# A chunked-state burst one matrix product earlier in each later token group, and one state cast on another engine

## The chip, the cores and the metric

The kernel runs on one core of a Trainium2 chip. The metric is the device time of one execution in microseconds (us); the figure for a kernel is the median over its runs.

## The reference

Two parts follow each other. The first is a retention layer (attention without a softmax, with a decay by distance), the second a two-layer network with a leaky rectifier:

```python
scores = scale * np.matmul(q, k.transpose(0, 1, 3, 2))      # 8 batches, 8 heads, 576 tokens, 64 wide
ret = np.matmul(scores * Dmat, v)                            # Dmat = gamma_h ** (i - j) for i >= j, else 0
x = ret.transpose(0, 2, 1, 3).reshape(4608, 512)
h = x @ w_in                                                 # 512 -> 2048
out = np.maximum(0.01 * h, h) @ w_out                        # 2048 -> 512
```

## The kernel before

**Units and groups.** The 4608 tokens are cut into 36 units of 128 tokens (two chunks of 64), and four units make a group of 512 tokens; there are nine groups, g = 0 to 8. Retention is computed by units in chunked form: inside a chunk with masked scores, across chunks with a running state of 64 x 64 per head. The two layers are computed by groups. In group g the matrix products of the layers are issued together with the retention of the units that later groups need. All orders on all engines are written out by hand: `tc.manual_schedule()` is on, and every engine runs its instructions in the order in which the program issues them.

**One unit's retention.** `step(u)` is `burst(u)` and then the preparation of later units. `burst(u)` issues, on TensorE, `scores(u)` (lines 221 and 230, 64x64 tiles into the one tile `sc`: the pool has a single buffer) and `outputs(u - 1)` (lines 305 and 316, into the one tile `ot`, again a single buffer). Then on VectorE `masks(u)` (line 248, reads `sc`), `state(u, 0)` and `state(u, 1)` (lines 270 to 275, read and sometimes write `sc`), on GpSimd `state_cast(u)` (line 287, the fp16 copy `st` of the states), on ScalarE `own(u - 1)` (line 372, reads `ot`), and on VectorE `add(u - 1)` (line 377, reads `ot` and `own`, writes the transposed layer input `xT`). So `scores(u)` may write `sc` only when `masks(u - 1)` and both `state(u - 1)` have read it, and `outputs(u - 1)` may write `ot` only when `add(u - 2)` has read it. `outputs(u - 1)` also reads the `st` of unit u - 1. After the burst `fetch(u + 4)` issues loads on SyncE's queue, and `ahead(u + 2)` casts k on ScalarE, q and v on GpSimd, and issues a transposing transfer on SyncE's queue. When u is a multiple of four, `ahead` has `sum_x` between the casts of q and v: four GpSimd operations (line 457) on the finished `xT` of the next group, whose results the next group's first layer reads.

**The layers.** Each is computed with seven half-size products where eight would be plain (a Strassen-like scheme), so sums of operands and of results are needed. `h_seven` is the first layer (its products are line 470, and the plain blocks `h_block` between them line 390); `seven` is the second one (products at line 590, 16 matmuls each). The second layer's plan in `others` is, for groups 2 and later:

```python
("p1", ..., False, lambda: give(0, 0, "p1")),
("p6", ..., True,  lambda: keep("u2", "p6", "k1")),
("p5", ..., True,  lambda: keep("v", "p5", "u2")),
("p7", ..., True,  lambda: give(1, 1, "p7", "v")),
("p5", ..., False, lambda: give(0, 1, "p5", "u2")),
("p7", ..., False, lambda: give(1, 0, "p7", "u2")),
```

`keep` (line 604) and the `give` with a `plus` (line 616) are VectorE additions that read a product's PSUM tile. The fifth product adds into the tile that `keep("v")` has read, and the sixth into the tile that `give(1, 1)` has read, so each must wait for that read. Ahead of the plan VectorE computes the last operand sums, `mix(g, 3, ...)` (line 571). `hooks[n]` is what is issued after product n and its reader, `hooks[0]` after the two `mix`. The four steps of group g are step 5 and step 6 inside the two `h_seven`, step 7 at `hooks[0]` and step 8 at another hook of `others`; "step n" is the step of unit 4g + n. Groups 2 to 7 have these steps; in group 7, step 8 is unit 36, which doesn't exist, and only `outputs(35)`, `own(35)`, `add(35)` and `sum_x(8)` are left of it. After the plan comes the next group's `h_seven`, in which the third product reads the results of `sum_x`.

**Unit 7.** The first units are written out one by one. Between `scores(7)` and `finish2(7)` (which is `outputs(7)`, `own(7)` and `add(7)`) stand the states of unit 7; `outputs(7)` reads both `st` of unit 6 (second half) and of unit 7 (first half).

Of the kernel before, what the change touches and what calls it, by code (L numbers as in the profile page):

```python
# [18 lines left out]
def kernel(  # L19
# [217 lines left out]
    def masks(u, aside=False):  # L237
        s16s[u] = b_pool.tile([P, 2, NP, CH], F16, name="s16")
        if aside:
            nc.scalar.copy(out=s16s[u], in_=sc_tiles[u][:, :, 0])  # L240
            nc.gpsimd.tensor_tensor(  # L241
                out=s16s[u],
                in0=s16s[u],
                in1=mask16.unsqueeze(1).unsqueeze(1).to_broadcast([P, 2, NP, CH]),
                op=MUL,
            )
            return
        nc.vector.tensor_tensor(  # L248
            out=s16s[u],
            in0=sc_tiles[u][:, :, 0],  # L250
            in1=mask_sb.unsqueeze(1).unsqueeze(1).to_broadcast([P, 2, NP, CH]),
            op=MUL,
        )
# [3 lines left out]
    def state(u, j):  # L257

        if j == 0:
            s32s[u] = a_pool.tile([P, 2, NP, CH], FP, name="s32")  # L260
            st16[u] = a_pool.tile([P, 2, NP, CH], F16, name="st16")
        c = (2 * u + j) % CB
        if c == CB - 1:
            carry[0] = None
            return
        st = sc_tiles[u][:, j, 1]
        to = s32s[u][:, j]
        scaled = c % (BLK // CH) == BLK // CH - 1
        if carry[0] is None:
            nc.vector.tensor_copy(out=to, in_=st)  # L270
        elif not scaled:
            nc.vector.tensor_tensor(out=to, in0=st, in1=carry[0], op=ADD)  # L272
        else:
            nc.vector.tensor_tensor(out=st, in0=st, in1=carry[0], op=ADD)  # L274
            nc.vector.tensor_tensor(
                out=to, in0=st,
                in1=gblk_sb.unsqueeze(2).to_broadcast([P, NP, CH]), op=MUL,
            )
        carry[0] = to

    def live(u, j):
        return (2 * u + j) % CB != CB - 1

    def state_cast(u, copy, js=(0, 1)):
        js = [j for j in js if live(u, j)]
        if len(js) == 2:
            copy(out=st16[u], in_=s32s[u])  # L287
        else:
            for j in js:
                copy(out=st16[u][:, j], in_=s32s[u][:, j])  # L290
# [85 lines left out]
    def add(u):  # L376
        nc.vector.tensor_tensor(  # L377
            out=x_of(u).rearrange("q (c g) t -> q c g t", g=2),
            in0=ot_tiles[u][:, :, NP : 2 * NP].rearrange("q g (c j) t -> q c g (j t)", j=2),
            in1=owns[u].rearrange("q (c g) j t -> q c g (j t)", g=2),  # L380
            op=ADD,
        )
# [23 lines left out]
    def h_block(g, f):  # L406
        hps = acc_pool.tile([P, 1, TOK], FP, name="acc")
        h_mm(hps, 0, g, f, slice(0, TOK))
        leaky(g_tile(g)[:, f : f + 1, :], hps)
# [149 lines left out]
    def mix(g, n, x):  # L559

        fs = slice(x * HF // 2, (x + 1) * HF // 2)
        if g not in sums:
            sums[g] = s_pool.tile([P, 2, HF, HT], F16, name="mix")
        s = sums[g]
        z, a, b, op = (
            (s[:, 0], g_part(g, 1, 0), g_part(g, 1, 1), ADD),
            (s[:, 1], s[:, 0], g_part(g, 0, 0), SUB),
            (g_part(g, 1, 0), g_part(g, 0, 0), g_part(g, 1, 0), SUB),
            (g_part(g, 0, 0), g_part(g, 0, 1), s[:, 1], SUB),
        )[n]  # L570
        nc.vector.tensor_tensor(out=z[:, fs], in0=a[:, fs], in1=b[:, fs], op=op)
# [97 lines left out]
    pool_copy, act_copy, dve_copy = nc.gpsimd.tensor_copy, nc.scalar.copy, nc.vector.tensor_copy  # L669
# [155 lines left out]
    def step(u, split=False):  # L825
        rest = burst(u, True, split)
        if u > 13:
            fetch(u + 4)
        ahead(u + 2, (lambda: sum_x(u // 4 - 1)) if u % 4 == 0 else None)
        return rest  # L830
# [53 lines left out]
    own(6)  # L884
    state_cast(6, act_copy, (1,))
    state(7, 0)
    masks(7)
    add(6)
    state_cast(7, dve_copy, (0,))
    state(7, 1)  # L890
    halves(1, (0, 5), (0, 6))
    finish2(7)
# [42 lines left out]
    first, others = seven(1)  # L935
# [10 lines left out]
    for g in range(2, NG):  # L946
        more = g < NG - 1
        first, others = seven(g, not more)

        def block(f):  # L950
            return lambda: h_block(g, f)

        def at_step(n, split=False):
            return (lambda: step(4 * g + n, split)) if more else None

        owed = h_seven(
            g, 0, [block(2), block(10), block(3), block(11)], at_step(5, True)
        )
        owed += [lambda: mix(g, 0, 0), lambda: mix(g, 1, 0)]
        for late in h_seven(  # L960
            g, 4, [block(6), block(7), block(14), first], at_step(6, True), owed
        ):
            late()
        mix(g, 2, 0)
        h_block(g, 15)
        for n in range(3):
            mix(g, n, 1)
        others({0: [at_step(7)], 4: [at_step(8)]} if more else {})


# [28 lines left out]
```

## Time and profile before

| | |
|---|---|
| median of 13 runs | 284.37 us (284.13 to 286.36) |
| profiled execution: its own time | 284.37 us |
| profiled execution: span of the program | 282.6 us |
| TensorE matmul busy | 274.4 us, 97% |
| VectorE (DVE) busy | 211.5 us, 75% |
| ScalarE (ACT) busy | 153.1 us, 54% |
| GpSimd (POOL) busy | 156.0 us, 55% |
| TensorE clock granted | full, in every slice |

A row of the timeline is "start us, us, engine line operation written<-read, shapes, count, [idle before <- what ended it]". Lines that follow each other of one kind are merged. PE is TensorE, DVE VectorE, ACT ScalarE, POOL GpSimd, SP SyncE. A matmul's row lasts until its modelled end, some 0.17 us after its successor has begun, so TensorE's progress is read from starts, not from ends. A VectorE instruction can begin some 0.08 us before the end of the one ahead of it.

### The profile page before, as it was taken

The page shows a single profiled execution, that of the slowest core. Times are in us where ns is not written, and L with a number is a line of the kernel's source. Part 1 is how long each engine was busy: PE and PEld are TensorE (multiplying, and loading weights), DVE is VectorE, ACT ScalarE, POOL GpSimd, SP SyncE. Part 2 cuts the span into 40 slices and gives each one's busy share as a digit, 9 for nine tenths or more (in the row PEclk, how much of TensorE's full clock was granted, in tenths as well). Part 3 has the DMA queues.
Part 4 walks back from the last instruction along what each step waited for, and adds up shares of the span by engine and source line. Part 5 has one row for each costly group of instructions (what it writes and reads, how often), then busy time and mean ns, then how long its engine had stood idle before and what let it go on. Part 6 is the DMA issues. An engine that isn't in the chain of part 4 may idle for free.

```text
span 282.6 us, 9823 instructions
## 1 busy us (share of the span) xinstructions
PE 274.4 (97%) x4229; PEld 205.6 (73%) x4229; DVE 211.5 (75%) x362; ACT 153.1 (54%) x282; POOL 156.0 (55%) x173
## 2 busy tenths in 40 slices
PE   7889999999999999999999999999999999999994
PEld 3568888745876787678867886788678867886683
DVE  2875688988866887689777986788688767865772
ACT  3766787633237733774277427752775277416610
POOL 8969755944459507950795069607951693051000
PEclk9999999999999999999999999999999999999999
DMA  8999999998999767987698669966996251012004
GB/s 221 297 245 205 291 207 315 232 198 195 237 266 287 167 137 107 281 191 173 144 272 184 151 116 296 189 152 142 249 208 152 50 179 39 2 74 77 0 3 148
DMA packets 123100, 50.04 MB, mean 177 GB/s; under 512 B 112048, under 2 KB 116784, under 8 KB 123056
## 3 DMA queue, kind: packets, MB, share of 16 engines
q1 hardware_dynamic: 116032, 37.23, 57.6%
q0 software_dynamic: 6736, 12.06, 17.7%
q8 instruction: 33, 0.54, 0.8%
q10 hardware_dynamic: 288, 0.11, 0.1%
q14 instruction: 11, 0.09, 0.1%
HBM read 36.81 MB, written 9.44 MB: 164 GB/s over the span
## 4 chain that ended last, share of the span: by engine, by line
PE 90%; DVE 6%; DMA 2%; issue 1%; ACT 0%; POOL 0%; DVEq 0%; POOLq 0%
PE acc L590 35%; PE acc L390 27%; PE acc L470 15%; PE acc L527 5%; PE sc L221 3%; DMA t<-in_q_dram 2%; PE ot L305 2%; PE ot L316 2%; PE sc L230 2%; DVE s L248 1%; DVE s L272 1%; PE acc L202 1%; DVE qk L177 1%; DVE st L290 1%; DVE sc L274 0%
## 5 line engine op out<-in xcount | busy, mean ns | idle before, releaser
L390 PE MATMUL acc<-xT,w_in 128*128 128x256 f16 (+2 forms) x496 | 88.6, 318 | 0.1
L590 PEld LDWEIGHTS <-gt 128*128 128x128 f16 x640 | 61.3, 98 | 8.5 <-ACT gt L404 0.8
L404 ACT ACTIVATE gt<-acc 128x512 f16<-128x512 f32 x102 | 58.4, 597 | 14.2 <-PE acc L390 13.5
L390 PEld LDWEIGHTS <-w_in 128*128 128x128 f16 x496 | 45.4, 98 | 17.8 <-issue 0.2
L590 PE MATMUL acc<-w_out,gt 128*128 128x256 f16 x384 | 46.3, 273 | 0.2 <-ACT gt L404 0.2
L372 ACT COPY own<-ot 128x512 f32<-128x512 f32 x33 | 19.3, 586 | 41.1 <-PE ot L316 40.9
L287 POOL CAST st<-s 128x512 f16<-128x512 f32 x21 | 12.8, 610 | 48.9 <-DVE s L272 31.2
L177 POOL TENSOR_TENSOR qk<-t,cs 128x512 f16<-128x512 f32 x28 | 30.7, 1096 | 0.1
L181 POOL TENSOR_TENSOR v<-t,cs 128x512 f16<-128x512 f32 x28 | 30.7, 1098 | 0.0
L590 PE MATMUL acc<-w_mix,gt 128*128 128x256 f16 x256 | 30.6, 273 | 0.0
L590 PE MATMUL acc<-w_mix,mix 128*128 128x256 f16 x256 | 29.3, 273 | 0.0
L404 ACT ACTIVATE gt<-h 128x512 f16<-128x512 f32 x42 | 25.7, 629 | 5.7 <-DVE h L481 5.3
L470 PEld LDWEIGHTS <-w_sum 128*128 128x128 f16 x224 | 21.9, 98 | 9.1 <-issue 1.1
L590 PEld LDWEIGHTS <-mix 128*128 128x128 f16 x256 | 25.0, 98 | 3.0
L377 DVE TENSOR_TENSOR xT<-ot,own 128x512 f16<-128x512 f32 x33 | 22.5, 681 | 3.0 <-ACT own L372 3.0
L481 DVE TENSOR_TENSOR h<-acc,u 128x512 f32<-128x512 f32 x28 | 19.2, 684 | 6.4 <-PE acc L470 6.4
L241 POOL TENSOR_TENSOR s<-s,idle 128x512 f16<-128x512 f16 x12 | 13.9, 1156 | 16.9 <-ACT s L240 16.9
L174 ACT CAST qk<-t 128x512 f16<-128x512 f32 x36 | 22.5, 625 | 1.1 <-DMA t<-in_k_dram 0.9
L470 PE MATMUL acc<-x_sum,w_sum 128*128 128x256 f16 x168 | 22.9, 272 | 0.0
L481 DVE TENSOR_TENSOR u<-acc,k 128x512 f32<-128x512 f32 x14 | 9.7, 690 | 17.4 <-PE acc L470 14.8
L470 PEld LDWEIGHTS <-w_in 128*128 128x128 f16 x168 | 16.3, 97 | 7.1 <-DVE h L481 0.8
L488 ACT COPY k<-acc 128x512 f32<-128x512 f32 x14 | 8.2, 585 | 22.1 <-issue 16.8
(77 smaller groups left out, 434.2 us busy)
## 6 DMA issues: line engine op xcount, KB each, us to landing
out_dram<-osb SPq DMA_DIRECT2D x17, 512.0 KB, 3.8
t<-in_k_dram SPq DMA_DIRECT2D x24, 256.0 KB, 3.7
t<-in_q_dram SPq DMA_DIRECT2D x23, 256.0 KB, 4.2
t<-in_v_dram SPq DMA_DIRECT2D x22, 256.0 KB, 4.8
t<-in_v_dram POOLq DMA_DIRECT2D x10, 256.0 KB, 6.4
t<-in_q_dram POOLq DMA_DIRECT2D x9, 256.0 KB, 5.7
t<-in_k_dram POOLq DMA_DIRECT2D x8, 256.0 KB, 7.4
w_in<-in_moe_w_in_dram POOLq DMA_DIRECT2D x8, 256.0 KB, 6.8
```

The lines of the kernel that those rows point to most:

```text
L174: nc.scalar.copy(out=qk16[u][:, 1], in_=t32[u, 1])
L177: eng.tensor_tensor(out=qk16[u][:, 0], in0=t32[u, 0], in1=decay(u, 0), op=MUL)
L181: eng.tensor_tensor(out=v16[u], in0=t32[u, 2], in1=decay(u, 1), op=MUL)
L241: nc.gpsimd.tensor_tensor(out=s16s[u], in0=s16s[u], in1=mask16.unsqueeze(1).unsqueeze(1).to_broadcast([P, 2, NP, CH]), op=MUL,)
L372: nc.scalar.copy(out=owns[u], in_=ot_tiles[u][:, :, 0:NP].rearrange("q j c t -> q c j t"))
L377: nc.vector.tensor_tensor(out=x_of(u).rearrange("q (c g) t -> q c g t", g=2), in0=ot_tiles[u][:, :, NP : 2 * NP].rearrange("q g (c j) t -> ...
L390: nc.tensor.matmul(out=hps[:, n, :], lhsT=w_in16[:, c, f * P : (f + 1) * P], rhs=xT[g][:, c, ts], start=(c == 0), stop=(c == NP - 1),)
L404: nc.scalar.activation(out=out, in_=in_, func=mybir.ActivationFunctionType.Lrelu)
L470: nc.tensor.matmul(out=r[name][:, n, :], lhsT=lhs[:, c, n * P : (n + 1) * P], rhs=rhs[:, c, :], start=fresh and n == 0 and c == 0, stop=c ...
L481: nc.vector.tensor_tensor(out=r[name], in0=r[a], in1=r[b], op=ADD)
L527: nc.tensor.matmul(out=ys[tb], lhsT=g_t[0][:, f, tb * P : (tb + 1) * P], rhs=w_out16[:, f, :], start=(f == 0), stop=(f == NF - 1),)
L590: nc.tensor.matmul(out=r[name][tb][:, 0, :] if apart else r[name][0][:, tb, :], lhsT=lhs[:, f, tb * P : (tb + 1) * P], rhs=rhs[:, f, :], s ...
```

## The change

Two edits. In the loop over groups 2 to 8, step 8 goes from the hook after the fourth product of the second layer to the hook after the third. In the part written out by hand, the fp16 cast of the first state of unit 7 goes from VectorE, behind `masks(7)` and `add(6)`, to ScalarE, ahead of them.

```diff
     own(6)
     state_cast(6, act_copy, (1,))
     state(7, 0)
+    state_cast(7, act_copy, (0,))
     masks(7)
     add(6)
-    state_cast(7, dve_copy, (0,))
     state(7, 1)
     halves(1, (0, 5), (0, 6))
     finish2(7)
...
         for n in range(3):
             mix(g, n, 1)
-        others({0: [at_step(7)], 4: [at_step(8)]} if more else {})
+        others({0: [at_step(7)], 3: [at_step(8)]} if more else {})
```

Each engine's order changes in this way. On TensorE the burst of step 8 (64 matmuls of 64x64) stands ahead of the fourth product's 16 matmuls instead of behind them. On VectorE `give(1, 1)` stands behind the burst's masks, two states and addition instead of ahead of them; the two `keep` stay ahead of the burst. On ScalarE, GpSimd and SyncE's queue the order in the loop stays as it was. For unit 7 VectorE has one instruction less and ScalarE one more.

## The prediction

> **What bounds the kernel now.** I read the page first. TensorE is busy nearly all the time, VectorE three quarters of it, and the clock is full.
>
> ```profile
> span 282.6 us, 9823 instructions
> ...
> PE 274.4 (97%) x4229; PEld 205.6 (73%) x4229; DVE 211.5 (75%) x362; ACT 153.1 (54%) x282; POOL 156.0 (55%) x173
> ...
> PEclk9999999999999999999999999999999999999999
> ...
> PE 90%; DVE 6%; DMA 2%; issue 1%; ACT 0%; POOL 0%; DVEq 0%; POOLq 0%
> ```
>
> The fourth line is the chain that ended last: 90% TensorE. So a moved burst pays only where it takes a wait off TensorE, and costs what new waits it puts there. TensorE's matmul count doesn't change.
>
> Next I read the windows view over the second layer, from the first `mix(g, 3)` to `give(0, 1)`, in groups 2 to 5, and for comparison a stretch of the first layer (columns: stretch, its length, busy time of each engine with instructions).
>
> ```profile
> 100.10:110.70 10.60, 10.60 (x156) 9.35 (x155) 10.19 (x18) 2.69 (x6) 3.68 (x5) 1.00 0.62 91
> 128.70:139.20 10.50, 10.50 (x156) 9.25 (x155) 10.10 (x18) 2.67 (x5) 3.73 (x5) 1.00 0.58 131
> 157.30:167.80 10.50, 10.50 (x156) 9.26 (x154) 10.13 (x18) 2.63 (x5) 3.64 (x5) 1.00 0.59 112
> 185.70:196.20 10.50, 10.50 (x156) 9.26 (x154) 10.10 (x18) 2.70 (x6) 3.70 (x5) 1.00 0.57 129
> ...
> 110.00:120.00 10.00, 10.00 (x130) 6.71 (x128) 6.09 (x11) 6.54 (x12) 9.92 (x11) 1.00 1.04 258
> ```
>
> The third figure after the length is VectorE: 10.10 of 10.50 us. VectorE is full just where the burst is moved, and has slack elsewhere. Last, the timeline of group 3 there (step 7 is unit 19, step 8 unit 20), VectorE's rows and then TensorE's:
>
> ```profile
> 133.37 0.42 DVE L275 TENSOR_TENSOR s<-sc,cs 128x256 f32<-128x256 f32 x1
> 133.72 0.68 DVE L377 TENSOR_TENSOR xT<-ot,own 128x512 f16<-128x512 f32 x1
> 134.31 0.68 DVE L604 TENSOR_TENSOR u<-acc,k 128x512 f32<-128x512 f32 x1
> 135.10 0.69 DVE L604 TENSOR_TENSOR v<-acc,u 128x512 f32<-128x512 f32 x1
> 135.88 0.69 DVE L616 TENSOR_TENSOR osb<-acc,v 128x512 f32<-128x512 f32 x1
> 136.49 0.68 DVE L248 TENSOR_TENSOR s<-sc,cs 128x512 f16<-128x512 f32 x1
> 137.09 0.87 DVE L272 TENSOR_TENSOR s<-sc,s 128x256 f32<-128x256 f32 x2
> 137.87 0.68 DVE L377 TENSOR_TENSOR xT<-ot,own 128x512 f16<-128x512 f32 x1
> ```
>
> ```profile
> 133.43 1.91 PE L590 MATMUL acc<-w_mix,gt 128*128 128x256 f16 x16
> 135.26 0.32 PE L221 MATMUL sc<-qkT 64*64 64x64 f16 x16
> 135.41 0.30 PE L230 MATMUL sc<-v,qk 64*64 64x64 f16 x16
> 135.54 0.30 PE L305 MATMUL ot<-s,v 64*64 64x64 f16 x16
> 135.67 0.31 PE L316 MATMUL ot<-qkT,st 64*64 64x64 f16 x16
> 135.91 1.92 PE L590 MATMUL acc<-w_out,gt 128*128 128x256 f16 x16
> 137.66 1.91 PE L590 MATMUL acc<-w_mix,gt 128*128 128x256 f16 x16
> ```
>
> The reader is to see three things. The fourth product begins at 133.43, which is where the burst is to go. At that moment VectorE hasn't yet done `state(19, 1)` (to 133.79) and `add(18)` (133.72 to 134.40), which free `sc` and `ot`. And the burst at 135.26 has all it needs in the order as it is.
>
> **The moved burst, group 3.** Spacings from starts: a product takes 1.75 us (135.91 to 137.66), 1.83 ahead of a burst (133.43 to 135.26); scores to outputs 0.28; outputs to the next product 0.37. Without waits the moved scores would start at 133.43 + 0.08 = 133.51, outputs at 133.79, the fourth product at 134.16. How fast TensorE goes on after such a wait I take from two bursts that stand one product apart at 70 us: there `state` ended at 70.26 and scores began at 70.41 (0.15), `add` ended at 70.86 and outputs began at 70.91 (0.05). So scores start at 133.79 + 0.15 = 133.94, outputs at the later of 134.22 and 134.40 + 0.05 = 134.45. The cast of `st` (to 134.54) is wanted by the second half of the far outputs, at about 134.65: in time. The fourth product starts at 134.45 + 0.37 = 134.82, 0.66 late.
>
> Then VectorE: `v` ends at 135.79; the burst's masks follow at once, at 135.71 with the usual overlap instead of 136.49 (0.78 earlier), since `give(1, 1)` no longer stands ahead. `add(19)` goes from 137.87 to 137.09, and `give(1, 1)` behind it runs 137.69 to 138.38. On TensorE the fifth product starts at 134.82 + 1.75 = 136.57 (it needs `v`: there), the sixth would at 138.32 but needs `give(1, 1)`: 138.38 + 0.05 = 138.43. The next group starts at 140.18, where it now starts at 139.41: 0.77 later.
>
> What it gains: `sum_x` follows `add` and the q cast on GpSimd, so it too comes 0.78 earlier, and the third product of the next `h_seven` waits for it now. The block ahead of that product takes 0.87 us elsewhere, but in groups 2 to 7 it lasts 1.01, 0.93, 1.06, 0.91, 0.86 and 0.86: waits of 0.14, 0.06, 0.19, 0.04, 0 and 0. With the next group late and `sum_x` early, all go. Net for group 3: 0.77 - 0.06 = 0.71.
>
> **The other groups,** by the same steps (fourth product's start T; `add` of step 7 ends; outputs start; `give(1, 1)` ends; next group's start now and then). Group 2: T 104.84, `sc` free 105.34, `add` 105.94, outputs 105.99, fourth product 106.36; `give` ends 109.93, so the sixth starts 109.98 instead of 109.86; 110.88 becomes 111.73, +0.85 - 0.14 = 0.71. Group 4: T 161.99, `add` 162.49, outputs 162.54, fourth product 162.91; three state operations make `give` end at 167.07, so the sixth waits from 166.41 to 167.12; 167.97 becomes 168.87, +0.90 - 0.19 = 0.71. Group 5: T 190.47, `add` 190.95, fourth product 191.37, `give` 195.41, sixth 195.46; 196.46 becomes 197.21, +0.75 - 0.04 = 0.71. That the four agree is no accident: now and then VectorE's one sequence sets the end. Group 6: one state operation less in step 7, `add` ends at 218.84 with outputs due at 219.15, `give` at 222.82 with the sixth due at 223.02: 0. Group 7: only outputs, due 247.15, `add` 247.71, outputs 247.76, all behind 0.59 late and no wait to gain: 252.79 becomes 253.38, +0.59. Sum: 4 x 0.71 + 0.59 = 3.43 us. Each group's VectorE sequence starts behind a leaky rectifier of that group (0.58 us idle before the first `mix`), so it moves with TensorE and doesn't catch up.
>
> **What else moves.** Step 8's own copy (0.59), the k cast (0.62) and GpSimd's casts stand in the same order and only come earlier; ScalarE sat idle 5.4 us ahead of that copy. SyncE's three loads and one transposing transfer of step 8 come up to 1.75 us earlier, with no transfer overtaken in the queue; their data are wanted one or more steps later, so 0. If the DMA share (0.6 in these windows) made them collide, GpSimd's casts would be late, with a whole step of cover.
>
> **The cast of unit 7.** Now `outputs(7)` waits for it: that run of line 316 lasts 0.47 us where the like lasts 0.32. On ScalarE the cast takes 0.41 (its row for this shape) and fits at 43.0 to 43.4, ahead of a rectifier that starts at 43.48 and waits for TensorE anyway. Gain 0.15, cost 0; if it pushed that rectifier, 0.1 lost at most.
>
> **Total:** 3.43 - 0.15 = +3.28. The profiled execution's own time, 284.37, is the median, so 287.65; I say 287.6.
>
> **Two rules of the Trainium skill against these rows.** "Perfetto Trace Analysis", section Identifying the Most-Contended Engine, takes an engine's occupancy over the window as a fair measure of its load. Over the span VectorE's 75% would leave a quarter free, the burst's 64 matmuls would find their tiles free, and the sum would be -0.43 - 0.15 = -0.6. The windows say 96%, and the stage decides. "TensorE: Matmul & The Clock Gate", section The HAM clock gate, halves TensorE's clock after an idle window of some 3.4 us, and its oscillation section tells of micro-idling that does it too. In this trace TensorE sits idle 0.65 us ahead of 15.8 and 0.51 ahead of 10.1, and PEclk stays at 9. I take no loss; by the rule a throttled window per stalled group would be an estimated 3.4/2 x 5 = 8.5 us more.
>
> **Rivals.** (a) VectorE keeps up: if `add` and `give(1, 1)` came 0.7 us earlier, as in group 6, no wait arises, `sum_x` is early, and the kernel goes to 284.4 - 0.6 = 283.8. It decides from the point where `add` of step 7 ends before T + 0.36. Against it: five of six groups miss that (group 7, without scores, T + 0.08) by 0.12 to 0.74 us. (b) Only the wait inside the burst counts, because `give(1, 1)` isn't in the sixth product's way: fourth products late by 0.79, 0.66, 0.19, 0.17, 0 and 0.59, less 0.43, 0.15 and the 0.06 that group 2's fifth product waits now: +1.8, 286.1. (c) The clock: 296. (d) As forecast, but each wait costs 0.15 more than I took, some seven waits: 288.7.
>
> **How the numbers follow.** Forecast with small deviations 0.70; (b) 0.11; (d) 0.08; (c) 0.02; (a) 0.09. Measurement tells about 0.3%, 0.85 us, from no change; (a) lies inside, with 0.03 beyond. So faster 0.03, same 0.06, slower 0.91. The range 286.1 to 288.8 holds the forecast, (b)'s value and (d).
>
> **What would show it.** Right: fourth products late behind line 305 waiting for DVE L377, sixth behind L616 in groups 2, 4 and 5, none in group 6; no wait for POOL x_sum; line 316 of unit 7 back at 0.32 us; each of groups 2 to 5 longer by 0.7. Wrong: outputs starting at T + 0.36 in every group, or an order of VectorE with masks ahead of `keep`.

## Result and profile after

The changed kernel takes 287.31 us (median of 11 runs, 287.07 to 289.17), the kernel before 284.42 us beside it: ratio 1.0108, 95% interval 1.009 to 1.0127, or 2.9 us more. The page of the profile after:

```profile
span 285.4 us, 9823 instructions
...
PE 275.0 (96%) x4229; PEld 206.0 (72%) x4229; DVE 211.7 (74%) x361; ACT 153.3 (54%) x283; POOL 154.1 (54%) x173
...
PEclk9999999999999999999999999999999999999999
...
PE 66%; DVE 25%; issue 3%; ACT 3%; DMA 2%; POOL 0%; DVEq 0%; POOLq 0%
```

The span is 2.8 us longer and TensorE's busy time only 0.6: the rest is idle time at full clock. The last line is the chain that ended last: VectorE's share of it was 6% before and is 25% now. The timeline of group 3, TensorE's rows and then VectorE's (the whole lies 0.34 us later than in the profile before when the first `mix(g, 3)` starts):

```profile
134.28 0.32 PE L221 MATMUL sc<-qkT 64*64 64x64 f16 x16 [0.36 <-DVE s L275]
134.41 0.32 PE L230 MATMUL sc<-v,qk 64*64 64x64 f16 x16
134.79 0.32 PE L305 MATMUL ot<-s,v 64*64 64x64 f16 x16
134.92 0.32 PE L316 MATMUL ot<-qkT,st 64*64 64x64 f16 x16
135.16 1.92 PE L590 MATMUL acc<-w_mix,gt 128*128 128x256 f16 x16
136.92 1.91 PE L590 MATMUL acc<-w_out,gt 128*128 128x256 f16 x16
138.76 1.91 PE L590 MATMUL acc<-w_mix,gt 128*128 128x256 f16 x16
140.50 0.60 PE L470 MATMUL acc<-xT,w_in 128*128 128x256 f16 x4
```

```profile
133.71 0.42 DVE L275 TENSOR_TENSOR s<-sc,cs 128x256 f32<-128x256 f32 x1
134.05 0.68 DVE L377 TENSOR_TENSOR xT<-ot,own 128x512 f16<-128x512 f32 x1
134.65 0.68 DVE L604 TENSOR_TENSOR u<-acc,k 128x512 f32<-128x512 f32 x1
135.44 0.69 DVE L604 TENSOR_TENSOR v<-acc,u 128x512 f32<-128x512 f32 x1
136.04 0.68 DVE L248 TENSOR_TENSOR s<-sc,cs 128x512 f16<-128x512 f32 x1
136.64 0.87 DVE L272 TENSOR_TENSOR s<-sc,s 128x256 f32<-128x256 f32 x2
137.43 0.68 DVE L377 TENSOR_TENSOR xT<-ot,own 128x512 f16<-128x512 f32 x1
138.03 0.68 DVE L616 TENSOR_TENSOR osb<-acc,v 128x512 f32<-128x512 f32 x1
```

Scores wait for line 275 (ends 134.13, scores at 134.28: 0.15). Scores to outputs takes 0.51 instead of 0.28: outputs wait for line 377 (ends 134.73, outputs at 134.79: 0.06). The sixth product starts 1.84 us behind the fifth instead of 1.75, because `give(1, 1)` ends at 138.71. And VectorE waits for no other engine from its first row to its last; its longest gap there is 0.11 us, ahead of the `keep` that reads what the one before it wrote.

TensorE's starts give the length of each group in two parts: the second layer from the end of its first product (the start of the row behind it) to the next group's first layer, and that first layer up to the same place in the next group. Worked out from the timelines:

| us | group 2 | 3 | 4 | 5 | 6 | 7 |
|---|---|---|---|---|---|---|
| second layer, before | 13.32 | 13.27 | 13.27 | 13.29 | 13.28 | 13.01 |
| second layer, after | 14.15 | 14.03 | 14.15 | 14.03 | 13.27 | 13.60 |
| longer | 0.83 | 0.76 | 0.88 | 0.74 | -0.01 | 0.59 |
| next first layer, before | 15.26 | 15.29 | 15.20 | 15.04 | 15.00 | 13.57 |
| next first layer, after | 15.00 | 15.00 | 15.00 | 15.00 | 15.00 | 13.56 |

The sum is +3.79 - 0.80 = 3.0 us from the start of group 2's first layer (82.53 us before, 82.29 after) to the end of VectorE's last addition (279.34, 282.12).

### The profile page after: what moved, and what is told of

Read it like the earlier page. It is cut to its first block, busy times and chain, and to the rows that moved or that the text cites. A ratio compares the mean times of both kernels' runs of the same rounds, so it can differ in the third digit from the quotient of the medians.

```text
span 285.4 us, 9823 instructions
## 1 busy us (share of the span) xinstructions
PE 275.0 (96%) x4229; PEld 206.0 (72%) x4229; DVE 211.7 (74%) x361; ACT 153.3 (54%) x283; POOL 154.1 (54%) x173
## 4 chain that ended last, share of the span: by engine, by line
PE 66%; DVE 25%; issue 3%; ACT 3%; DMA 2%; POOL 0%; DVEq 0%; POOLq 0%
PE acc L390 23%; PE acc L590 22%; PE acc L470 15%; DVE w_mix L552 4%; DVE mix L571 3%; DVE s L248 3%; DVE gt L571 3%; ACT gt L404 2%; DVE xT L377 2%; DMA t<-in_q_dram 2%; PE sc L221 2%; DVE s L272 2%; DVE h L481 1%; PE ot L305 1%; DVE sc L274 1%
## 5 line engine op out<-in xcount | busy, mean ns | idle before, releaser
L177 POOL TENSOR_TENSOR qk<-t,cs 128x512 f16<-128x512 f32 x28 | 29.8, 1064 | 0.1
L181 POOL TENSOR_TENSOR v<-t,cs 128x512 f16<-128x512 f32 x28 | 29.4, 1049 | 0.0
```

Source lines behind the costliest of these rows:

```text
L177: eng.tensor_tensor(out=qk16[u][:, 0], in0=t32[u, 0], in1=decay(u, 0), op=MUL)
L181: eng.tensor_tensor(out=v16[u], in0=t32[u, 2], in1=decay(u, 1), op=MUL)
```

## Experiments

The theory: the moved burst waits for VectorE, which is full in this stage, and in groups 2 to 5 VectorE's one sequence up to `give(1, 1)` sets the end. Rivals: the wait inside the burst alone costs; `give(1, 1)` behind the burst costs; the burst's place costs by itself; the cast shares in the loss.

The startup differs between the ten profiled executions: group 2's first layer began between 82.3 and 82.8 us in six of them and between 84.3 and 85.3 in four, and this does not follow the edits (the last section says what three of the four show). So beside each ratio stands the time from there to the end of VectorE's last addition, called "from group 2 on": 196.81 us before and 199.83 after, which is free of the startup. Each such figure comes from one profiled execution, and single waits of some 0.2 us come and go in it.

### The two edits apart

```diff
     state(7, 0)
-    state_cast(7, act_copy, (0,))
     masks(7)
     add(6)
+    state_cast(7, dve_copy, (0,))
```

> The burst moved, the cast of unit 7 left on VectorE. Theory (the moved burst waits for VectorE, the cast is a gain of 0.15 us of its own): 0.15 us above the changed kernel, so about 3.0 us above the kernel before; groups 2 to 5 and 7 longer, group 6 not. Rival (the cast on ScalarE delays the layers and shares the loss): clearly below the changed kernel, at most 2.5 us above before.

Measured: ratio 1.0136 (1.009 to 1.0183). From group 2 on 200.10 us, with second layers of 14.16, 14.04, 14.17, 14.04, 13.27 and 13.61: the changed kernel's within 0.02. So all of the loss comes with the moved burst. The 0.15 us of the cast can't be read from the ratios, whose intervals overlap.

```diff
-        others({0: [at_step(7)], 3: [at_step(8)]} if more else {})
+        others({0: [at_step(7)], 4: [at_step(8)]} if more else {})
```

> The cast of unit 7 on ScalarE, the burst where it was. Theory: the run of line 316 of unit 7 goes from 0.47 to 0.32 us and nothing else moves, so 0.15 us (0.05%) below the kernel before. Rival (the cast is in the rectifiers' way): 0 to 0.3 us above before.

Measured: ratio 0.9988 (0.9966 to 1.001), not told from 1. From group 2 on 196.71. The run of line 316 of unit 7 lasts 0.30 us. But it lasts 0.30 with the move alone too, where the cast is on VectorE. In the kernel before, the cast met a load being issued by GpSimd; with the move alone this load came 2 us ahead of it. VectorE's and GpSimd's timelines, first of the kernel before, then of the move alone:

```profile
44.06 0.49 DVE L290 CAST st<-s 128x256 f16<-128x256 f32 x1
```

```profile
43.57 0.89 POOL L134 DMA_DIRECT2D t<-in_k_dram  x1 [1.65 <-ACT st L290]
```

```profile
46.66 0.28 DVE L290 CAST st<-s 128x256 f16<-128x256 f32 x1
```

```profile
44.70 0.89 POOL L134 DMA_DIRECT2D t<-in_k_dram  x1 [1.64 <-ACT st L290]
```

So the wait that the second edit takes away is there when the cast lasts 0.49 us and not when it lasts 0.28. A third profile with this cast on VectorE, the kernel before with less work (below), has 0.28 and 0.30 again: there the next such load is issued 0.14 us behind the cast's start. That an issuing load stretches a cast that begins behind it is read from these overlaps alone, and no run isolates it.

### VectorE's work ahead of the burst put off

```diff
-            mix(g, 3, 0)
-            mix(g, 3, 1)
+            if g < 2:
+                mix(g, 3, 0)
+                mix(g, 3, 1)
             for f in hooks.get(0, ()):
                 f()
+            if g >= 2:
+                mix(g, 3, 0)
+                mix(g, 3, 1)
```

> The changed kernel with the two mix(g, 3) of groups 2 and later issued behind step 7 instead of ahead of it, so that VectorE frees sc and ot 1.29 us earlier, while it has the same instructions to do up to give(1, 1). Theory (in groups 2 to 5 the one sequence of VectorE up to give(1, 1) sets the end, in group 7 the wait inside the burst): the wait inside the burst goes in every group, but the sixth product of groups 2 to 5 waits instead, until the same moment as before the edit, and only group 7 gets its 0.6 us back: about 0.6 us below the changed kernel, 2.2 to 2.3 above before. Rival (the wait inside the burst is what costs): fourth products on time and with them the groups, 2.0 to 2.4 us below the changed kernel, 0.5 to 0.9 above before.

Measured: ratio 1.0272 (1.0221 to 1.0322), from group 2 on 204.59 us: slower than either said. TensorE's timeline of group 3 and, from that of all engines, two rows of VectorE and GpSimd:

```profile
135.54 0.30 PE L305 MATMUL ot<-s,v 64*64 64x64 f16 x16
135.91 1.92 PE L590 MATMUL acc<-w_mix,gt 128*128 128x256 f16 x16
138.53 1.91 PE L590 MATMUL acc<-w_out,gt 128*128 128x256 f16 x16 [0.70 <-DVE v L604]
141.11 1.91 PE L590 MATMUL acc<-w_mix,gt 128*128 128x256 f16 x16 [0.68 <-DVE osb L616]
```

```profile
134.85 2.23 DVE L571 TENSOR_TENSOR gt<-gt,mix 128x1024 f16<-128x1024 f16 x2
135.04 1.49 POOL L177 TENSOR_TENSOR qk<-t,cs 128x512 f16<-128x512 f32 x1
```

And one row of VectorE's timeline in group 6:

```profile
223.98 3.01 DVE L571 TENSOR_TENSOR gt<-gt,mix 128x1024 f16<-128x1024 f16 x2
```

The wait inside the burst is gone, and the group is longer all the same: that rival falls. What neither foresaw is that the two `mix` now run beside GpSimd's q cast and last 2.23 us instead of 1.29, and the cast 1.49 instead of 1.04. Those 0.94 us are what the second layers of groups 2 to 5 grew by over the changed kernel: 15.10, 14.97, 15.11 and 14.97 against 14.15, 14.03, 14.15 and 14.03. In group 6 the two `mix` meet both of GpSimd's casts, q and v, and last 3.01 us, 1.73 more than in the changed kernel; that group, where both expected no loss, lasts 14.84 us instead of 13.27, or 1.57 more, since VectorE had some 0.2 us in hand there. In group 7 no such cast stands beside the `mix`, and it is back at 13.01. So the sequence of VectorE sets the end also with the longer `mix` in it; the theory was right on the mechanism and wrong on the size, for want of this collision. The Trainium skill has it: "GPSIMD Engine Reference", section 1. Specifications, says that GpSimd's SBUF interfaces are shared with VectorE and contend when a VectorE instruction has two SBUF inputs, as these `mix` have. VectorE's additions that read PSUM kept their 0.68 us beside the v cast.

### give(1, 1) ahead of the burst's VectorE work

`burst_pe(u)` issues `scores(u)` and `outputs(u - 1)`; `step(u, pe=False)` is the rest of the step.

```diff
-        others({0: [at_step(7)], 3: [at_step(8)]} if more else {})
+        n8 = 4 * g + 8
+        others(
+            {
+                0: [at_step(7)],
+                3: [lambda: burst_pe(n8)],
+                4: [lambda: step(n8, pe=False)],
+            }
+            if more
+            else {}
+        )
```

> The changed kernel with only TensorE's part of step 8 behind the third product; its work on the other engines (masks, states, addition, copies, loads) stays behind give(1, 1) of the fourth. Rival (give(1, 1) standing behind the burst's work is what costs): the sixth products no longer wait, 0.6 to 1 us below the changed kernel. Theory (TensorE is late wherever VectorE's sequence is late): the sixth products don't wait, but fourth products stay late by 0.8, 0.7, 0.2, 0.2, 0 and 0.6 us, give(1, 1) must now wait for the late fourth product with all of VectorE's work behind it, sum_x comes 0.75 to 0.9 us later than in the kernel before, and the next layer's third product waits for it by 0.3, 0.3, 0.9, 0.8, 0.3 and 0: about 4.4 us above before, 1.5 above the changed kernel.

Measured: ratio 1.0145 (1.0096 to 1.0195), from group 2 on 201.04 us, 4.2 above before and 1.2 above the changed kernel. No sixth product waits. The block ahead of the third product of the next first layer lasts 1.17, 1.17, 1.77, 1.64, 1.17 and 0.86 us, so the waits are 0.31, 0.31, 0.91, 0.78, 0.31 and 0, as the theory had them. In VectorE's timeline of group 4, and TensorE's behind it:

```profile
168.19 0.69 DVE L616 TENSOR_TENSOR osb<-acc,v 128x512 f32<-128x512 f32 x1 [0.99 <-PE acc L590]
```

```profile
175.00 0.27 PE L470 MATMUL acc<-x_sum,w_sum 128*128 128x256 f16 x1 [0.74 <-POOL x_sum L457]
```

VectorE idles 0.99 us for the late fourth product with its whole burst queued behind, and hands the delay to GpSimd's `x_sum`. The rival falls: without the wait for `give(1, 1)` the kernel is not faster. That the changed kernel's order is the better of the two rests on these profiled executions; the intervals of the two ratios overlap.

### VectorE's work taken away, with the burst in both places

```diff
-            mix(g, 3, 0)
-            mix(g, 3, 1)
+            if g < 2 or last:
+                mix(g, 3, 0)
+                mix(g, 3, 1)
```

> The changed kernel with the two mix(g, 3) of groups 2 to 7 left out (the fifth product then takes an unsummed operand), which takes 1.29 us of VectorE's work from ahead of the burst and nothing from TensorE. Theory (the moved burst costs because VectorE's sequence is full): add of step 7 ends 1.29 us earlier, ahead of the outputs in every group, give(1, 1) ends ahead of the sixth product, no wait is left, and sum_x is early: 0.6 to 1.1 us below the kernel before, so 3.4 to 4 below the changed one. Rival (a burst between the third and the fourth product costs TensorE by its place, by transfers or by PSUM traffic): still 2 us or more above before.

> The kernel before with the same two mix(g, 3) left out. Theory: the burst waits for nothing as it is, sum_x comes about 0.5 us earlier and its waits of 0.14, 0.06, 0.19 and 0.04 go: 0.4 to 0.8 us below the kernel before, and within 0.4 us of the other kernel with less work. Rival (by its place): 3 us faster than that one.

Both leave out these sums, so the second layers of groups 2 to 7 compute something else; TensorE's products stay. Measured: with the burst moved, ratio 0.997 (0.9951 to 0.999), from group 2 on 195.96 us; with the burst where it was, 1.0 (0.9981 to 1.002), 196.39 us. TensorE's and VectorE's timelines of group 3 with the burst moved:

```profile
133.18 0.32 PE L221 MATMUL sc<-qkT 64*64 64x64 f16 x16
133.32 0.30 PE L230 MATMUL sc<-v,qk 64*64 64x64 f16 x16
133.45 0.30 PE L305 MATMUL ot<-s,v 64*64 64x64 f16 x16
133.58 0.31 PE L316 MATMUL ot<-qkT,st 64*64 64x64 f16 x16
133.82 1.92 PE L590 MATMUL acc<-w_mix,gt 128*128 128x256 f16 x16
135.58 1.91 PE L590 MATMUL acc<-w_out,gt 128*128 128x256 f16 x16
137.32 1.91 PE L590 MATMUL acc<-w_mix,gt 128*128 128x256 f16 x16
```

```profile
132.17 0.68 DVE L377 TENSOR_TENSOR xT<-ot,own 128x512 f16<-128x512 f32 x1
...
136.15 0.68 DVE L616 TENSOR_TENSOR osb<-acc,v 128x512 f32<-128x512 f32 x1
137.52 0.69 DVE L616 TENSOR_TENSOR osb<-acc,u 128x512 f32<-128x512 f32 x1 [0.70 <-PE acc L590]
```

`add` ends at 132.85 and scores start at 133.18; `give(1, 1)` ends 0.49 us ahead of the sixth product. All waits are gone, the second layers are back at 13.27, 13.27, 13.27, 13.28, 13.27 and 13.01, and 1.29 us of VectorE's work per group was worth 3.9 us of the whole (199.83 to 195.96). The burst's place costs TensorE nothing: that rival falls. The second expectation was half missed: two of the four waits for `sum_x` stayed, behind groups 4 and 5 (blocks of 1.03 and 0.90 us), and the ratio shows no gain. With VectorE relieved the moved burst is 0.43 us ahead of the other order: 0.21 are these two waits, which the move takes away; the other 0.22 is one of the single waits that come and go, and is not the move's.

### The move in group 6 alone

```diff
-        others({0: [at_step(7)], 3: [at_step(8)]} if more else {})
+        others({0: [at_step(7)], 3 if g == 6 else 4: [at_step(8)]} if more else {})
```

> The changed kernel with the burst moved in group 6 alone. Theory: that group has one state operation less ahead of the burst, VectorE is in time, group 6 lasts as long as now (13.27 us from the end of its first layer's sums to the next group), and the whole is the kernel with the cast alone. Rival (by its place): 0.5 to 0.7 us longer in group 6.

Measured: group 6 lasts 13.27 us; from group 2 on 196.59 us, the cast alone 196.71; ratio 0.9983 (0.9968 to 0.9997). TensorE's timeline of group 6:

```profile
218.85 0.32 PE L221 MATMUL sc<-qkT 64*64 64x64 f16 x16
219.00 0.30 PE L230 MATMUL sc<-v,qk 64*64 64x64 f16 x16
219.13 0.30 PE L305 MATMUL ot<-s,v 64*64 64x64 f16 x16
```

Outputs follow scores by 0.28 us: one state operation less ahead of it, and VectorE is in time.

### What the move was worth, had another way

```diff
         if u < NU:
             cast_k(u)
+        if between is not None and first:
+            between(0)                     # x_sum 0 and 1
+        if u < NU:
             cast_q(u, nc.gpsimd)
         if between is not None:
-            between()
+            between(1 if first else None)  # x_sum 2 and 3; all four where first is not set
```

> The kernel with the cast of unit 7 on ScalarE and the burst where it was, and on GpSimd the first two operations of sum_x ahead of step 8's cast of q instead of behind it (1.04 us). Theory: the next layer's third product finds its operands 1.0 us earlier, the waits of 0.14, 0.06, 0.19 and 0.04 us go, and some of the waits for VectorE behind them; the q cast and its transposing transfer come 2.3 us later, which the 7 us to their reader cover: 0.5 to 0.9 us below the kernel before. Rival (the transfer is then late for step 6 of the next group): no faster or slower than before.

Measured: ratio 0.9977 (0.9961 to 0.9992), or 0.65 us below the kernel before; from group 2 on 196.15 us, 0.66 below. GpSimd's timeline and TensorE's, in which line 474 is the former 470:

```profile
138.40 1.15 POOL L461 TENSOR_TENSOR x_sum<-xT 128x512 f16<-128x512 f16 x1
139.63 1.16 POOL L461 TENSOR_TENSOR x_sum<-xT,x_sum 128x512 f16<-128x512 f16 x1
140.75 1.04 POOL L177 TENSOR_TENSOR qk<-t,cs 128x512 f16<-128x512 f32 x1
```

```profile
140.88 1.03 PE L390 MATMUL acc<-xT,w_in 128*128 128x512 f16 x4
141.75 1.04 PE L474 MATMUL acc<-x_sum,w_sum 128*128 128x256 f16 x8
```

The sums end 0.96 us ahead of their reader, the block lasts 0.87 us, all the waits for `sum_x` are gone, and the later q cast makes nobody wait. This version beats both kernels.

## Why the prediction was right

- **The wait inside the burst.** Right in all six groups: outputs wait for line 377 in groups 2 to 5 and 7, none waits in group 6. The restart times that it took from two bursts at 70 us, 0.15 and 0.05 us, were 0.15 and 0.06 in group 3.
- **The sixth product behind give(1, 1).** Right: in group 5 it starts 2.31 us behind the fifth instead of 1.75, a wait of 0.56 where 0.59 was worked out. TensorE's timeline:

```profile
192.88 1.92 PE L590 MATMUL acc<-w_mix,gt 128*128 128x256 f16 x16
194.63 1.91 PE L590 MATMUL acc<-w_out,gt 128*128 128x256 f16 x16
196.94 1.91 PE L590 MATMUL acc<-w_mix,gt 128*128 128x256 f16 x16 [0.40 <-DVE osb L616]
```

- **Sizes.** Second layers longer by 0.83, 0.76, 0.88, 0.74, -0.01 and 0.59, forecast 0.85, 0.77, 0.90, 0.75, 0 and 0.59. Less the wait for `sum_x` that each had, groups 2 to 5 lost 0.68 to 0.69 each, forecast 0.71.
- **The gain at sum_x.** All waits went, as said, and were 0.47 us from TensorE's starts (0.15, 0.07, 0.20 and 0.05) where 0.43 was forecast. But the first layers became 0.80 shorter. Most of the rest are single waits in first layers of the profile before, 0.21 us for VectorE at 146.5 and some 0.1 in a burst at 122.4. The 0.21 does not follow the move: it is there also in the move alone and with less work and the burst in its old place, and isn't there with the cast alone. What makes it come and go is open.
- **The cast.** The run of line 316 went from 0.47 to 0.30, 0.17 for the 0.15 forecast; but the edit's worth in another run isn't shown, since the wait needn't be there.
- **Total.** +3.28 forecast, 2.9 by the medians. From group 2 on, where the cast has no part, 3.43 was forecast and 3.0 measured; the 0.4 between them is nearly all in the first layers' extra gain, which the prediction did not have.
- **The two rules.** The occupancy over the whole span would have made the move free, and the stage decided. The clock stayed full through the waits of this stage, the longest of which was 0.5 us, and also through the 0.7 us waits with the two `mix` put off: 1.00 granted in every group's window. (What the prediction takes from the Trainium skill on micro-idling stands in "TensorE: Matmul & The Clock Gate", section A second HAM failure mode: psum-queue depth-cycling.) At the startup the clock did drop in some executions, as the last section shows.

## What to carry to other kernels

Ask of an engine how full it is in the stage that a change touches: at 75% over the span, VectorE was at 96% there, and moving TensorE's work ahead of what VectorE has yet to free only turned a product's cover into a wait. Where one engine's sequence is the bound, changing which of its instructions is waited for moves the wait from one place to the next; only less work in it, or a shorter path behind it, gives time back. The four short waits that an earlier burst could have taken away cost nothing to take away by an order on GpSimd, because nobody waited for the q cast that went behind them.

## What the hardware showed beside this

- Two fp16 VectorE subtractions with both inputs in SBUF took 2.23 us instead of 1.29 beside GpSimd's two-input multiplication, which itself took 1.49 instead of 1.04. The rows fit with their taking turns: in group 3 of the kernel with the two `mix` put off the multiplication began 0.19 us behind the first subtraction, and the second one ended 0.55 us behind the multiplication.
- The granted clock fell in the startup of three profiled executions (the cast alone, `give(1, 1)` ahead, and the kernel before with less work). Between 17 and 19 us it was 0.50 to 0.58, and the first layer's first two rows of eight 128x256 matmuls (line 390) took 1.61 to 1.89 us each where the profile before has 1.04 and 1.05. This is most of their late start of group 2. The kernel before with less work has the same startup as the kernel before, which kept the full clock. TensorE's wait just ahead was 0.66 to 0.71 us in these three, but 0.70 in the changed kernel too, which also kept it, so what decides is not shown. From the page of the cast alone:

```profile
PEclk9979999999999999999999999999999999999999
```

- In the move alone TensorE stopped for 0.95 us in the middle of 16 small matmuls at 44 us, and the profile names nothing that it waited for. TensorE's timeline:

```profile
44.80 0.28 PE L230 MATMUL sc<-v,qk 64*64 64x64 f16 x10 [0.95 <-issue]
```
